# LSH attention and an MLP on one core: transfers and weight loads as one server in the planner, and a new table of priorities

## The chip, the cores and the metric

One core of a Trainium2 chip runs the whole program in one launch. The metric is the device time of an execution in microseconds. TensorE is written PE, VectorE DVE, ScalarE ACT, GpSimd POOL; SyncE (SP) issues most transfers.

## The reference

q, k and v have the shape (4, 8, 768, 64): 4 batches, 8 heads. Each row of q and k gets a bucket from the signs of 6 projections; a query sees only the keys of its own bucket. The heads' outputs stand side by side as 3072 tokens of 512 numbers, which go through a two-layer MLP.

```python
q_bucket = sum((q @ proj > 0) * 2**arange(6));  k_bucket likewise
mask   = q_bucket[:, None] == k_bucket[None, :]
scores = where(mask, (q @ k.T) / 8, -1e9)
attn   = softmax(scores) @ v                  # by batch and head
x      = attn as (3072, 512)
r      = maximum(x @ w_in, 0)                 # w_in 512 x 2048
out    = (s * r*r + b) @ w_out                # w_out 2048 x 512
```

## The kernel before

Attention goes by visits, one for each batch and head (32), and each visit by three chunks of 256 queries: 96 slots. For each slot PE makes scores of all 768 keys (L657 or L659, the "lead"), DVE takes the maxima (L665), PE transposes them (L676, first 24 slots only), DVE reduces them (L678), PE transposes once more (L680), DVE writes the row of maxima (L687), and PE adds mask and maxima to the scores (L697 or L699, the "rest"). ACT takes the exponentials (L704), PE multiplies them with v (L727, or L729 and L730), ACT brings the result out of PSUM (L767, L769). Bank 4 of PSUM serves the transposes L676 and L680 and also the preparation of later visits: transposes of q and k (L477, L491), hashes (L515, L528 to L533), sums of v (L579, L615). None of these may write it until DVE has read what stands there.

Visits 0, 1, 4 and 7 (heads of mode "a" and "b") need no transfers between preparation and scores. The others do: after the hash (L533 or L529) DVE makes the bits (L545) and SP issues four transfers inside SBUF (`aq<-bq`, `bq<-aq`, `ks<-nat`, `aq<-nat`), and the lead L659 waits for the last. Two heads done, a quarter of a token's features goes to DRAM (`xd<-xsb`) and comes back laid out for the MLP (`xc<-xd`, L802).

The MLP (L815 and L832) of a chunk can start when all 8 heads of the chunk are there, from slot 23 on. From then on PE has matmuls that wait for nothing in attention. The weights come in as 32 loads of 512 KB on ACT's queue (`raw<-in_moe_w...`, L392), and in the first 28 slots ACT, DVE and POOL split each into two parts (L393 to L405).

No engine chooses at run time: each runs its instructions in a written order. That order comes from a planner in the file, `Plan.order`. Every step is added with an engine, a cost, what it reads and writes, a priority `pr`, and a `lag` after which its result can be used. The planner plays the engines forward by these costs and at each point takes the ready step of lowest priority number. `NUDGE` adds a number to the priority of each source site (91 of them) in each of up to five stretches of the program (`CUTS`). In the model before, SP's transfers follow each other on one server (`moved`), and ACT's weight loads are outside it: they take 0.1 us of ACT and land 5.0 us later, whatever else is under way.

Of the kernel before, what the change touches and what calls it, by code (L numbers as in the profile page):

```python
# [31 lines left out]
class Plan:  # L32
# [41 lines left out]
    def order(self):  # L74
        n = len(self.steps)
        sites = sorted({s[2].__code__.co_firstlineno for s in self.steps})
        pr = []
# [32 lines left out]
        while len(out) < n:  # L110
# [33 lines left out]
            if e == SP:  # L144
                moved = max(moved, start + cost) + lag
                end += moved - start - cost
            else:
                end += lag
# [28 lines left out]
HOP = {None: 0.0, PE: 0.2, DVE: 0.06, ACT: 0.06, POOL: 0.06, SP: 1.8}  # L177
SAME = {None: 0.0, PE: 0.2, DVE: 0.06, ACT: 0.06, POOL: 0.06, SP: 0.0}
# [10 lines left out]
def lsh_attention_moe(ctx: ExitStack, tc, q, k, v, proj, w_in, w_out, s, b, out):  # L189
# [34 lines left out]
    def dma(dst, src, r, w, pr, size=0):  # L224

        plan.add(SP, 0.7, lambda: nc.sync.dma_start(f32(dst()), f32(src())), r, w, pr, size / 2.6e5)
# [144 lines left out]
    def decode(u, pr):  # L371
# [20 lines left out]
        plan.add(ACT, 0.1, lambda: nc.scalar.dma_start(raw(), src.rearrange("p (n t) -> p n t", t=2)), KK("a") if u < PACE else [], rk + [("pace", u % PACE)], pr - 5, 5.0)  # L392
# [41 lines left out]
    def load(w, pr):  # L434
# [3 lines left out]
        if w >= BT:  # L438
            flat = NAT[x].rearrange("p t j d -> p (t j d)")
            for j in range(4):  # L440
                to = flat[j * SQ:(j + 1) * SQ].rearrange("r (t m e) -> r t m e", t=NT, e=SQ)
                z = (q, k)[j // 2][bb, h].rearrange("(m r t) (j e) -> j r t m e", r=SQ, t=NT, e=SQ)[j % 2]
                plan.add(SP, 0.7, lambda to=to, z=z: nc.sync.dma_start(to, z), [], [("nat", x, j)], pr, 0.9)
            return
        for j, z in enumerate((q, k)):
            to = NAT[x][:, :, j]
            plan.add(SP, 0.7, lambda to=to, z=z: nc.sync.dma_start(to, z[bb, h].rearrange("(p t) d -> p t d", t=NT)), [], [("nat", x, j)], pr, 0.9)
# [112 lines left out]
    def prep_values(w, pr):  # L560
# [4 lines left out]
        if w < NPL:  # L565
# [5 lines left out]
            plan.add(SP, 0.7, lambda: nc.sync.dma_start(EV[x][:, :, 0], vd), [], vk[0:1], pr, 0.9)  # L571
# [26 lines left out]
        def fetch(to, tk, vd):  # L598
            plan.add(SP, 0.7, lambda: nc.sync.dma_start(to, vd), [], [tk], pr, 0.9)
# [190 lines left out]
    def moe(bb, c):  # L790
        boxes = []
        pr = 1e5 + 100.0 * nu[0]
        for cc in range(NC_):
# [8 lines left out]
            plan.add(SP, 0.7, lambda box=box, src=src: nc.sync.dma_start(f32(box["t"]), f32(src)), [("xd", (bb, cc, c))], [("xc", r)], pr, 262144 / 2.6e5)  # L802
# [103 lines left out]
PACE = 2  # L906
# [130 lines left out]
```

## Time and profile before

| | us |
|---|---|
| median of 3 runs | 987.71 |
| lowest, highest | 985.8, 988.32 |
| the profiled execution's own time | 984.95 |
| its span, first to last instruction | 983.2 |

The busy shares are PE 98%, PEld (loading of PE's weights, beside PE) 88%, DVE 71%, ACT 72%, POOL 69%. The profile's rows give busy time by engine, windows of it, waits with what ended them, and the chain of work that ended last. A matmul of the exact heads (L657, and L727 of the first 27 slots) shows as two records in the trace for one instruction in the order.

### The profile page before, as it was taken

The numbers are of one execution on the slowest core, as the hardware profiler recorded it, in microseconds if no ns is written. First come the engines' busy times: TensorE is split into PE (matmuls) and PEld (weight loads), VectorE is DVE, ScalarE is ACT, GpSimd is POOL, SyncE is SP. The second block draws the span as 40 slices with busy tenths as digits, with TensorE's granted clock in tenths as the row PEclk, the third lists the DMA queues.
The fourth block names the chain that finished last, engine by engine and source line by source line (L and its number), as shares of the span: only waits on it lengthen the run. The fifth ranks groups of instructions, "written<-read, shape, count | busy, mean of one in ns | idle before, by whom it ended". The sixth has DMA issues, their size and how long they took to land.

```text
span 983.2 us, 17823 instructions
## 1 busy us (share of the span) xinstructions
PE 958.6 (98%) x6322; PEld 863.4 (88%) x6322; DVE 699.3 (71%) x1081; ACT 703.8 (72%) x1365; POOL 680.2 (69%) x641
## 2 busy tenths in 40 slices
PE   8999878999999999999999999999999999999998
PEld 7877667789999999999999999999999999989997
DVE  6678678878888898888898888888888876100000
ACT  4777667768888787878788788878887877433332
POOL 3677766588878786978788787869788788422222
PEclk9999999999999999999999999999999999999999
DMA  7574765642433442533433433533523310201100
GB/s 189 140 208 136 187 148 160 173 89 57 122 93 75 103 116 60 135 83 73 122 85 82 102 100 70 138 80 83 136 64 73 116 36 11 87 23 43 33 22 22
DMA packets 133680, 95.21 MB, mean 97 GB/s; under 512 B 101464, under 2 KB 106328, under 8 KB 133592
## 3 DMA queue, kind: packets, MB, share of 16 engines
q1 hardware_dynamic: 128248, 77.03, 31.2%
q10 hardware_dynamic: 5344, 17.05, 5.5%
q8 instruction: 50, 0.82, 0.3%
q14 instruction: 38, 0.31, 0.1%
HBM read 50.40 MB, written 18.87 MB: 70 GB/s over the span
## 4 chain that ended last, share of the span: by engine, by line
PE 94%; ACT 2%; DVE 2%; DMA 1%; issue 1%; POOL 0%; DVEq 0%; ACTq 0%; SPq 0%; POOLq 0%
PE bank L815 28%; PE bank L832 27%; PE bank L659 7%; PE bank L727 6%; PE bank L699 6%; PE bank L729 5%; PE bank L730 5%; PE bank L657 3%; PE bank L680 1%; PE bank L762 1%; PE bank L528 1%; PE bank L529 1%; PE bank L697 1%; ACT ex L704 1%; PE bank L515 1%
## 5 line engine op out<-in xcount | busy, mean ns | idle before, releaser
L815 PE MATMUL bank<-xc,w 128*128 128x256 f32 x2304 | 341.7, 283 | 0.0
L723 POOL TENSOR_TENSOR hl<-et,hl 128x512 fp32r<-128x512 f32 x207 | 267.5, 1320 | 82.3 <-ACT hl L722 73.3
L815 PEld LDWEIGHTS bank<-xc,w 128*128 128x128 f32 x2304 | 309.4, 190 | 8.2
L832 PE MATMUL bank<-w,ghb 128*128 128x512 f32 x768 | 251.8, 397 | 0.0
L823 POOL TENSOR_TENSOR glb<-rb,ghb 128x512 fp32r<-128x512 f32 x96 | 124.7, 1299 | 106.6 <-ACT ghb L822 97.5
L665 DVE TENSOR_REDUCE mx<-bank 128x256 f32<-128x1536 f32 x96 | 167.9, 1749 | 8.2 <-PE bank L659 4.8
L704 ACT ACTIVATE et<-bank 128x512 f32<-128x512 f32 x234 | 129.2, 626 | 49.8 <-PE bank L699 31.1
L749 DVE TENSOR_REDUCE zb<-et 128x256 f32<-128x1536 f32 x69 | 120.7, 1750 | 48.0 <-ACT et L704 43.9
L832 PE MATMUL bank<-w,glb 128*128 128x512 f32 x384 | 152.5, 398 | 0.0
L832 PEld LDWEIGHTS bank<-w,ghb 128*128 128x128 f32 x768 | 134.3, 189 | 17.8
L722 ACT CAST hl<-et 128x512 fp32r<-128x512 f32 x207 | 125.4, 668 | 0.3
L820 ACT ACTIVATE rb<-bank 128x512 f32<-128x512 f32 x96 | 56.9, 593 | 89.6 <-PE bank L815 88.8
L659 PE MATMUL bank<-aq,ks 84*128 84x256 f32 x504 | 110.1, 304 | 4.4 <-DMA aq<-nat 3.3
L729 PE MATMUL bank<-hl,vs 128*128 128x256 f32 x414 | 109.0, 286 | 0.0
L730 PE MATMUL bank<-hl,vs 128*128 128x256 f32 x414 | 107.4, 282 | 0.0
L659 PEld LDWEIGHTS bank<-aq,ks 84*128 84x128 f32 x504 | 80.1, 191 | 12.0 <-ACT w L399 3.0
L729 PEld LDWEIGHTS bank<-hl,vs 128*128 128x128 f32 x414 | 78.0, 188 | 7.9
L832 PEld LDWEIGHTS bank<-w,glb 128*128 128x128 f32 x384 | 72.3, 188 | 13.8 <-POOL glb L823 0.2
L730 PEld LDWEIGHTS bank<-hl,vs 128*128 128x128 f32 x414 | 78.4, 189 | 6.6
L769 ACT ACTIVATE xpb<-bank,vmn 64x256 f32<-64x256 f32 x96 | 44.9, 468 | 49.5 <-PE bank L730 29.8
L840 DVE SCALAR_TENSOR_TENSOR osb<-bank,misc,bcs 128x512 f32<-128x512 f32 x22 | 16.2, 743 | 89.4 <-PE bank L832 89.1
L699 PE MATMUL bank<-bq,ks 128*128 128x256 f32 x504 | 76.7, 287 | 0.0
(144 smaller groups left out, 1571.1 us busy)
## 6 DMA issues: line engine op xcount, KB each, us to landing
xd<-xsb SPq DMA_DIRECT2D x48, 256.0 KB
xc<-xd SPq DMA_DIRECT2D x48, 256.0 KB
raw<-in_moe_w_in_dram ACTq DMA_DIRECT2D x16, 512.0 KB
raw<-in_moe_w_out_dram ACTq DMA_DIRECT2D x16, 512.0 KB
vn<-in_v_dram SPq DMA_DIRECT2D x34, 192.0 KB
out_dram<-osb SPq DMA_DIRECT2D x22, 256.0 KB
ks<-aq SPq DMA_DIRECT2D x28, 192.0 KB
ks<-bq SPq DMA_DIRECT2D x28, 192.0 KB
```

The source lines that it names most:

```text
L659: nc.tensor.matmul(o, ks[0:HR + NR, 0, kt], aq[0:HR + NR, cs], start=m == 0, stop=m == 1, skip_group_check=True)
L665: dve(S * TPC, lambda: nc.vector.tensor_reduce(t, sc, AX.XY, ALU.max), [("b", b) for b in pb], [tk], pr, 1.75)
L699: nc.tensor.matmul(o, ks[:, 1, kt], bq[:, cs], start=False, stop=m == 1, skip_group_check=True)
L704: act(512, lambda p=p, z=z: nc.scalar.activation(et(z) if plain(i) else pairs(z), bank[:, pb[p]] if plain(i) else bank[:, pb[p]].rearrange ...
L722: act(512, lambda z=z, y=y: nc.scalar.copy(HL[2 * y].rearrange("p (m n) -> p m n", n=CH), pairs(z)), [("e", z)], [("hl", 2 * y)], pr, 0.05)
L723: pool(512, lambda z=z, y=y: nc.gpsimd.tensor_tensor(HL[2 * y + 1].rearrange("p (m n) -> p m n", n=CH), pairs(z), f32(HL[2 * y]).rearrange ...
L729: nc.tensor.matmul(av, VS[x][:, kt], HL[2 * y][:, ms], start=(kt == 0), stop=False)
L730: nc.tensor.matmul(av, VS[x][:, kt], HL[2 * y + 1][:, ms], start=False, stop=(kt == NT - 1))
L749: dve(S * TPC, lambda: nc.vector.tensor_reduce(ZB, es, AX.XY, ALU.add), [("e", z) for z in range(NE)], ["zb"], pr, 1.75)
L815: nc.tensor.matmul(hp, wt[("wi", n, cc)][:, m % 2, fs], xc[:, m // 2, :], start=(cc == 0 and m == 0), stop=(cc == NC_ - 1 and m == 2))
L823: pool(2 * CH, lambda r=r, gh=gh, gl=gl: nc.gpsimd.tensor_tensor(gl, r, f32(gh), ALU.subtract), [rk, hk], [lk], MP)
L832: nc.tensor.matmul(bank[:, 6 + t, :], (gh, gh, gl)[n][:, ts], wt[("wo", f)][:, n % 2], start=(f == 0 and n == 0), stop=(f == NF - 1 and n ...
```

## The change

In the planner, a step with a lag, on whatever queue, now passes one server: `moved` runs on by the step's lag, and the result is there 1.3 us (`LAND`) after. Costs and lags of all transfers are new numbers: of a weight load 0.33 us to issue and 2.2 us of service, of a 256 KB transfer 0.45 us and about 0.78 us, of the small ones 0.36 to 0.7 us and 0.7 to 1.1 us. The table `NUDGE` has other values at nearly every place. Nothing else differs: the same instructions with the same operands, in another order. The line numbers of the changed file are smaller by one.

```diff
             free[e] = start + cost
             end = start + cost + HOP[e]
-            if e == SP:
+            if lag:
                 moved = max(moved, start + cost) + lag
-                end += moved - start - cost
-            else:
-                end += lag
+                end = moved + LAND
...
+LAND = 1.3
...
     def dma(dst, src, r, w, pr, size=0):
-        plan.add(SP, 0.7, lambda: nc.sync.dma_start(f32(dst()), f32(src())), r, w, pr, size / 2.6e5)
+        plan.add(SP, 0.45 if size > 2e5 else 0.68, lambda: nc.sync.dma_start(f32(dst()), f32(src())), r, w, pr, size / (3.4e5 if size > 2e5 else 2.5e5) + 0.01)
...
-        plan.add(ACT, 0.1, lambda: nc.scalar.dma_start(raw(), src.rearrange("p (n t) -> p n t", t=2)), KK("a") if u < PACE else [], rk + [("pace", u % PACE)], pr - 5, 5.0)
+        plan.add(ACT, 0.33, lambda: nc.scalar.dma_start(raw(), src.rearrange("p (n t) -> p n t", t=2)), KK("a") if u < PACE else [], rk + [("pace", u % PACE)], pr - 5, 2.2)
...
 NUDGE = {
-    0: {0: -3.8, 1: -12.8, 2: 5.9, 3: 23, 4: -30},
+    0: {0: 30, 1: -20.8, 2: 7.3, 3: -18.6, 4: -8.3},
...
```

Three places show what moves. The first is PE, from the second hash of visit 6 (batch 0, head 6; its tiles are `aq1`, `bq1`, `ks1`) to its first lead. `eva`, `vs5` are values of visits 4 and 5, `ks0` the keys of visit 5, `nat1` holds q and k of visit 7. Before:

```order
L533 MATMUL bank_64<-bq1_71,pjs_134 24x384
L727 MATMUL bank_64<-et_81,vs5_793 128x256 x3
L676 MATMUL bank_64<-ident_117,mx_88 128x128 x2
L727 MATMUL bank_64<-et_81,vs5_793 128x256
L680 MATMUL bank_64<-ident_117,nmt_93 8x128
L477 MATMUL bank_64<-ident_117,nat1_67 128x128 x3
L699 MATMUL bank_64<-bq0_70,ks0_72 128x256 x6
L659 MATMUL bank_64<-aq1_69,ks1_73 128x256 x2
```

In the changed kernel (L532 is before's L533, and so on):

```order
L532 MATMUL bank_64<-bq1_71,pjs_134 24x384
L658 MATMUL bank_64<-aq0_68,ks0_72 128x256 x6
L726 MATMUL bank_64<-ex5_87,eva_75 128x256
L675 MATMUL bank_64<-ident_117,mx_88 128x128 x2
L679 MATMUL bank_64<-ident_117,nmt_93 8x128
L726 MATMUL bank_64<-et_81,vs5_804 128x256 x2
L698 MATMUL bank_64<-bq0_70,ks0_72 128x256 x2
L578 MATMUL bank_64<-misc_102,vn_74 64x1
L698 MATMUL bank_64<-bq0_70,ks0_72 128x256 x4
L726 MATMUL bank_64<-et_81,vs5_804 128x256 x4
L675 MATMUL bank_64<-ident_117,mx_88 128x128 x2
L658 MATMUL bank_64<-aq1_69,ks1_73 128x256 x6
```

Between hash and lead there are now seven value matmuls where there were four, and six leads of visit 5 that stood earlier. The transposes of `nat1` (L477), which stood directly behind L680, are gone from here; two value matmuls stand behind L679.

The second is ACT in the same stretch: the weight loads 21 and 22 (`raw21`, `raw22`) and the exponentials (`ex0` to `ex2`) of slot 16. Before:

```order
L392 DMA raw21_235<-in_moe_w_out_dram 128x1024
L393 ACTIVATE osb_101<-raw20_234 128x512
L769 ACTIVATE xpb_96<-bank_64,vmn_92 64x256
L394 ACTIVATE raw20_234<-raw20_234 128x512
L767 ACTIVATE zpb_91<-bank_64 64x256
L392 DMA raw22_236<-in_moe_w_out_dram 128x1024
L480 ACTIVATE eqb_78<-bank_64,misc_102 128x384
L704 ACTIVATE ex0_82<-bank_64 128x512
L704 ACTIVATE ex1_83<-bank_64 128x512
L704 ACTIVATE ex2_84<-bank_64 128x512
L399 CAST w19_1197<-osb_101 128x512
L480 ACTIVATE eqb_78<-bank_64,misc_102 128x384
```

In the changed kernel:

```order
L391 DMA raw21_235<-in_moe_w_out_dram 128x1024
L398 CAST w18_1172<-osb_101 128x512
L703 ACTIVATE ex0_82<-bank_64 128x512
L557 ACTIVATE vmn_92<-bank_64 64x1
L703 ACTIVATE ex1_83<-bank_64 128x512
L703 ACTIVATE ex2_84<-bank_64 128x512
L392 ACTIVATE osb_101<-raw20_234 128x512
L768 ACTIVATE xpb_96<-bank_64,vmn_92 64x256
L398 CAST w19_1198<-osb_101 128x512
L766 ACTIVATE zpb_91<-bank_64 64x256
L393 ACTIVATE raw20_234<-raw20_234 128x512
L391 DMA raw22_236<-in_moe_w_out_dram 128x1024
```

Load 22 stood ahead of the three exponentials, with four instructions between it and load 21; now it stands behind them, with ten between. A copy of a weight (L398) now stands ahead of the exponentials and a mean (L557) among them.

The third is PE where the MLP starts, in slots 23 and 24 (`xc0_0_0` to `xc0_0_3` are the four parts of the first chunk). Before:

```order
L815 MATMUL bank_64<-xc0_0_0_240,w0_364 128x256 x3
L815 MATMUL bank_64<-xc0_0_1_241,w1_398 128x256 x3
L815 MATMUL bank_64<-xc0_0_2_242,w2_432 128x256
L727 MATMUL bank_64<-ex4_86,evb_76 128x256 x2
L680 MATMUL bank_64<-ident_117,nmt_93 8x128
L727 MATMUL bank_64<-ex5_87,evb_76 128x256 x2
L815 MATMUL bank_64<-xc0_0_2_242,w2_432 128x256 x2
L699 MATMUL bank_64<-bq0_70,ks0_72 128x256 x6
L528 MATMUL bank_64<-aq1_69,pjs_134 56x384
L529 MATMUL bank_64<-bq1_71,pjs_134 24x384
L815 MATMUL bank_64<-xc0_0_3_243,w3_461 128x256 x2
L659 MATMUL bank_64<-aq0_68,ks0_72 128x256 x2
```

In the changed kernel:

```order
L814 MATMUL bank_64<-xc0_0_0_240,w0_356 128x256 x3
L814 MATMUL bank_64<-xc0_0_1_241,w1_397 128x256 x3
L814 MATMUL bank_64<-xc0_0_2_242,w2_447 128x256 x3
L726 MATMUL bank_64<-ex3_85,evb_76 128x256 x2
L726 MATMUL bank_64<-ex4_86,evb_76 128x256 x2
L726 MATMUL bank_64<-ex5_87,evb_76 128x256
L679 MATMUL bank_64<-ident_117,nmt_93 8x128
L726 MATMUL bank_64<-ex5_87,evb_76 128x256
L698 MATMUL bank_64<-bq0_70,ks0_72 128x256 x6
L527 MATMUL bank_64<-aq1_69,pjs_134 56x384
L528 MATMUL bank_64<-bq1_71,pjs_134 24x384
L658 MATMUL bank_64<-aq0_68,ks0_72 128x256 x2
```

Before, the first MLP matmuls stood in four places among attention's; now nine stand together, and the next, which read `xc0_0_3`, come after 14 rows of attention.

## Rows read from the trace of the kernel before

**Rows 1.** The page, busy time by engine: us (share of the span), instructions.

```profile
...
PE 958.6 (98%) x6322; PEld 863.4 (88%) x6322; DVE 699.3 (71%) x1081; ACT 703.8 (72%) x1365; POOL 680.2 (69%) x641
```

**Rows 2.** Windows: length, busy us (instructions) by engine, PEclk, DMA share, GB/s.

```profile
...
8.00:185.00 177.00, 157.49 (x839) 126.14 (x837) 135.84 (x209) 126.61 (x252) 117.13 (x114) 0.99 0.62 169
185.00:979.00 794.00, 793.96 (x5444) 730.62 (x5442) 557.88 (x842) 575.68 (x1112) 560.12 (x518) 1.00 0.31 80
979.00:984.00 5.00, 0.38 (x2) 0.00 (x0) 1.23 (x3) 0.00 (x0) 0.00 (x0) 0.82 0.30 105
```

**Rows 3.** Waits of TensorE, 8 to 185 us: total us, times, longest.

```profile
...
PE bank L659 <- DMA aq<-nat: 3.3, 2, 2.8
PE bank L697 <- DVE zhl L687: 2.5, 4, 1.1
PE bank L727 <- ACT ex L704: 2.4, 4, 1.4
PE bank L579 <- DVE bq L687: 1.4, 3, 0.6
PE bank L680 <- DVE nmt L678: 1.2, 3, 0.5
...
PE bank L477 <- DVE bq L687: 1.2, 2, 0.6
...
PE bank L515 <- DVE bq L687: 0.7, 2, 0.5
...
PE bank L657 <- ACT ex L704: 0.6, 2, 0.3
...
PE bank L491 <- DVE bq L687: 0.5, 1, 0.5
```

**Rows 4.** Chain that ended last, 110 to 117 us: start, us, what.

```profile
...
113.50 2.43 DMA aq<-nat
...
116.06 0.95 PE bank L659 x6
```

**Rows 5.** The same chain, 124 to 136 us.

```profile
...
125.22 0.18 PE bank L533
...
126.69 0.23 PE bank L676 x2
...
128.10 4.03 DMA aq<-nat
...
132.37 0.77 PE bank L659 x2
```

**Rows 6.** Timeline of ScalarE, 124 to 133 us: start, us, instruction.

```profile
...
127.39 0.33 ACTq L392 DMA_DIRECT2D raw<-in_moe_w_out_dram  x1
...
129.46 1.56 ACT L704 ACTIVATE ex<-bank 128x512 f32<-128x512 f32 x3
```

**Rows 7.** Windows around the wait in rows 5 (columns as in rows 2).

```profile
...
123.00:127.30 4.30, 4.30 (x25) 3.47 (x23) 3.60 (x6) 3.21 (x6) 2.14 (x3) 1.00 0.71 198
127.30:132.40 5.10, 1.59 (x12) 1.19 (x11) 2.48 (x6) 4.08 (x8) 3.21 (x3) 0.99 0.58 158
132.40:135.80 3.40, 3.40 (x12) 3.04 (x13) 1.95 (x2) 1.39 (x3) 1.21 (x2) 0.51 0.55 87
```

**Rows 8.** Lines of ScalarE, 8 to 185 us: count | busy us, mean ns | idle before.

```profile
...
L399 ACT CAST w<-osb 128x512 fp32r<-128x512 f32 x28 | 17.3, 618 | 3.1 <-POOL osb L397 3.1
...
L769 ACT ACTIVATE xpb<-bank,vmn 64x256 f32<-64x256 f32 x23 | 10.8, 468 | 15.7 <-PE bank L727 15.5
...
L521 ACT COPY eka<-eqa 12x768 f32<-12x768 f32 x2 | 1.7, 828 | 0.4 <-DVE eqa L517 0.3
```

**Rows 9.** Lines of VectorE, 8 to 185 us.

```profile
...
L517 DVE TENSOR_SCALAR eqb<-bank,misc 44x384 f32<-44x384 f32 x4 | 2.7, 670 | 2.4 <-PE bank L515 2.3
```

**Rows 10.** The same chain, 190 to 195 us, back-to-back matmuls.

```profile
...
190.37 1.08 PE bank L815 x9
...
191.90 2.76 PE bank L727 x12
```

More of the change, by code (lines that the diff above doesn't have):

```diff
@@ L442, in load @@
                 z = (q, k)[j // 2][bb, h].rearrange("(m r t) (j e) -> j r t m e", r=SQ, t=NT, e=SQ)[j % 2]
-                plan.add(SP, 0.7, lambda to=to, z=z: nc.sync.dma_start(to, z), [], [("nat", x, j)], pr, 0.9)
+                plan.add(SP, 0.68, lambda to=to, z=z: nc.sync.dma_start(to, z), [], [("nat", x, j)], pr, 0.7)
             return
@@ L446, in load @@
             to = NAT[x][:, :, j]
-            plan.add(SP, 0.7, lambda to=to, z=z: nc.sync.dma_start(to, z[bb, h].rearrange("(p t) d -> p t d", t=NT)), [], [("nat", x, j)], pr, 0.9)
+            plan.add(SP, 0.7, lambda to=to, z=z: nc.sync.dma_start(to, z[bb, h].rearrange("(p t) d -> p t d", t=NT)), [], [("nat", x, j)], pr, 1.0)
     nfill = [0]
@@ L570, in prep_values @@
                 pool(1, lambda: nc.gpsimd.memset(EV[x][:, :, 1], 1.0), [], vk[1:2], pr, 0.5)
-            plan.add(SP, 0.7, lambda: nc.sync.dma_start(EV[x][:, :, 0], vd), [], vk[0:1], pr, 0.9)
+            plan.add(SP, 0.6, lambda: nc.sync.dma_start(EV[x][:, :, 0], vd), [], vk[0:1], pr, 1.1)
             if w > 1:
@@ L598, in fetch @@
         def fetch(to, tk, vd):
-            plan.add(SP, 0.7, lambda: nc.sync.dma_start(to, vd), [], [tk], pr, 0.9)
+            plan.add(SP, 0.36, lambda: nc.sync.dma_start(to, vd), [], [tk], pr, 0.8)
         def sums(j, to, tk):
@@ L801, in moe @@
             src = xd[(bb, cc, c)]
-            plan.add(SP, 0.7, lambda box=box, src=src: nc.sync.dma_start(f32(box["t"]), f32(src)), [("xd", (bb, cc, c))], [("xc", r)], pr, 262144 / 2.6e5)
+            plan.add(SP, 0.36, lambda box=box, src=src: nc.sync.dma_start(f32(box["t"]), f32(src)), [("xd", (bb, cc, c))], [("xc", r)], pr, 1.0)
             boxes.append((box, ("xc", r)))
```

180 rows, old and new, of the table NUDGE are left out of this document.

## Prediction

> **What bounds the kernel now.** I read the page first: PE is busy for 98% of the span, the other engines for about 70% [rows 1], so PE is the bound on average. The windows say where it isn't. From 185 us, when the MLP has started, to 979 us PE is idle for 794.00 - 793.96 = 0.04 us [rows 2]; no order of the same matmuls gains there, and one only loses if it opens a gap. From 8 to 185 us, batch 0 of attention, PE is idle for 177.00 - 157.49 = 19.5 us [rows 2], while no other engine is busy for more than 136 of the 177 us: no engine is full, each waits for another in turn. So the change is worth what it does to these 19.5 us, and to one stretch after a wait in which PE ran at the lower of its two clock levels. The view of the waits splits the 19.5: 3.3 us for a transfer, 7.5 us for DVE's steps behind the transposes of bank 4 (2.5 + 1.4 + 1.2 + 1.2 + 0.7 + 0.5), 3.0 us for exponentials (2.4 + 0.6) [rows 3], the rest in small pieces. The chain shows where the transfer is late, the windows around it what the clock then did.
>
> **The change part by part.** The instructions are the same, so nothing is saved or added in work; only waits change. The planner's costs act through the order alone, and I judge them by what the order now puts between a producer and its user, in PE time by the durations of records: 0.12 us for a score or MLP matmul, 0.23 us a record and two records, so 0.46 us, for a value matmul of an exact head [rows 10].
>
> *The transfer behind the hash.* Visit 6's second hash ends at 125.22 + 0.18 = 125.40 us, its first lead starts at 132.37 [rows 5]: 6.97 us, filled with 3.2 us of PE work in the order (four value matmuls 1.84, two transposes 0.23 [rows 5], the rest of visit 5 0.72, four short transposes about 0.4). The last transfer took 4.03 us [rows 5], the same transfer of visit 5 took 2.43 us [rows 4]. What differs is weight load 22, issued at 127.39 us [rows 6], 0.71 us ahead of it. In the new order that load stands behind the exponentials of slot 16, which began at 129.46 us [rows 6] in the old run, so the small transfer should be nearer to 2.43: the way takes 6.97 - 1.60 = 5.4 us. PE's filling becomes 5.3 us (seven value matmuls 3.2, twelve score matmuls 1.4, transposes and a sum 0.7). Left: 0.1 of 2.8 us. Visit 5's wait was the other 0.5 us of the 3.3 [rows 3]; its filling goes from about 4.0 to 6.2 us in the order, so it goes. Gain 3.2 us; at best 3.3, at worst 0, if the next late thing (below) ends in the same place.
>
> A rule of the Trainium skill speaks against the planner's picture here. In "DMA: Bandwidth & Descriptors", section "Queues, rings and completion order", each DMA engine takes turns between the queues it has work for, packet by packet; SP's transfers then share with a load of ACT's queue, and don't stand behind the whole of it as the one server has them. The trace can't settle it: sharing would be the 1.6 us between 2.43 and 4.03; a server would make the small transfer wait for 512 KB at 198 GB/s [rows 7], 2.6 us, less the 0.71 already gone, 1.9 us. By the one the term is as above, by the other 0.3 us larger, which is not there to be gained. So the rule changes no sum at this place.
>
> *The clock.* After that wait PE's granted clock is 0.51 for 3.4 us [rows 7], the 1.2 GHz level; before it PE had been idle for 5.10 - 1.59 = 3.5 us of 5.1. PE is busy all through it, so half of it is lost: 1.7 us. With no long wait ahead of it I take the whole 1.7; at worst 0, or another such stretch elsewhere (+1.7).
>
> *Bank 4.* Behind L680 the row of maxima must be written before a bank-4 step or the rest may run. In the order of the first 24 slots, such a step stands directly behind L680 in 9 slots before (0, 8, 11, 15 to 18, 21, 22) and in 4 now (0, 6, 7, 10); L680 directly behind L676 in 2 before (0, 18), in 3 now (0, 16, 20). The waits for L687 are 2.5 + 1.4 + 1.2 + 0.7 + 0.5 = 6.3 us [rows 3], those of L680 for L678 1.2 [rows 3]. Scaled by the places they become 6.3 x 4/9 = 2.8 and 1.2 x 3/2 = 1.8: gain 3.5 - 0.6 = 2.9 us. Best 3.5, worst 0, when another input of the same step ends as late.
>
> *Exponentials.* Two counts oppose each other. Value matmuls with under 1 us of PE work since the rest they depend on: 9 slots before, 3 now, which scales the 3.0 us to 1.0, a gain of 2.0. But ACT has 20 other instructions between the three exponentials of a slot where it had 8, over 24 slots; scaled by those the 3.0 us become 7.5, a loss of 4.5. PE's own waits are nearest to the first count, ACT's queue to the second: I take 0 and keep both ends.
>
> *The start of the MLP.* Nine of its matmuls run, then 14 rows of attention stand alone, some 7.5 us by the durations above. PE is idle 11% of batch 0 (19.5 of 177), so 0.8 us is lost there; 0 to 1.5.
>
> *Visit 7.* Between its second hash and its first lead PE has 2.3 us of work, where it had 10.3. The way is 0.67 on DVE [rows 9] and 0.83 on ACT [rows 8] behind an exponential that itself takes some 0.6 (1.56 for three [rows 6] at closer spacing): 2.1 us and the hops. I take 0.3 lost; up to 1.8 when a queued step on DVE and on ACT come first (0.6 each [rows 8]).
>
> All other edits are priced at nothing: from visit 9 on every hash has over 13 us of PE work ahead of its lead in both orders (25 us from visit 12 on), so a later landing is hidden by the MLP. Were that cover gone, each visit would pay what visit 6 paid, 2.8 us.
>
> **The sum.** -3.2 - 1.7 - 2.9 + 0 + 0.8 + 0.3 = -6.7 us. Against the profiled execution, 984.95 us (a span of 983.2 and 1.75 around it), that is 978.3. That execution is 2.76 us below the median of the runs, 987.71, and below all three; runs of the changed kernel will be compared by medians, so the forecast is 987.71 - 6.7 = 981.0.
>
> **Rivals.** *The gain is given back at the next wait.* In the stretch of the long wait ACT is busy for 4.08 of 5.10 us [rows 7]: it is what comes late next, and PE's value matmuls wait for its exponentials instead of the transfer. Likewise behind L680. Then the clock's 1.7 and, as I choose, a fourth of the 3.2 are left: -2.5, 985.2. For it: all engines but PE are at 70% or more in batch 0, each PE wait there is short, and 19.5 us are spread over many places. Against: the order adds filling at nearly every place named.
>
> *ACT's queue turns it round.* The 12 further instructions ahead of exponentials cost PE what they last: six are L769 at 0.47 us [rows 8], and at that mean 12 make 5.6 us. And an L769 waits for PE's values: 15.7 us of idle time for 23 of them [rows 8], 0.68 each, 4.1 for six, during which the exponentials behind it stand. 9.7 us, all on PE's path if the filling doesn't cover it: 987.71 - 6.7 + 9.7 = 990.7. It decides from 6.7 us on, two thirds of it. Against: rest to value matmul has more PE work between than before in most slots, which is just what would cover a later exponential.
>
> *More than I count.* The shorter waits of batch 0 that I priced at nothing (19.5 - 3.3 - 7.5 - 3.0 = 5.7 us) shrink as the bare places of bank 4 do (11 in all become 7), by 4/11, 2.1 us, and the exponentials by their 2.0: -10.8, 976.9.
>
> *The planner's server is the wrong picture.* If queues share the engines, the order guards against delays that aren't there, and the costs are as good or bad as the old ones: 987.7, no change; it adds to the first rival's chance.
>
> **How the numbers follow.** Forecast (978 to 984.5) 0.50; more 0.12; given back, or the planner's picture worthless, 0.23; turned round 0.15. A measurement of this kernel can tell 0.3%, 3 us, from no change. The forecast and the larger gain are over that, save a little at the upper end: faster 0.63. Of the third case most lies within: same 0.22. Slower 0.15. The range leaves out the upper part of the turned case and the far end of the large gain: 975.5 to 989.
>
> **What would show it.** In the profile of the changed kernel: windows from 8 us to the start of the MLP with about 14 us of PE idle instead of 19.5; no wait of L658 for `aq<-nat` above 0.5 us; the granted clock at 1.00 throughout batch 0; the waits for DVE's L686 and L677 about 5 us. The forecast is wrong if waits of PE for L703 grow past 6 us, if the wait at visit 6 is there again under another name, or if a gap opens behind the start of the MLP.

## The result and the profile after

The changed kernel takes 999.85 us (median of 4 runs, 999.45 to 1001.34), the kernel before 988.02 (median of 4, 985.8 to 989.03): ratio 1.0114, 95% interval 1.010 to 1.0128. It is slower by 1.1%; 981.0 was forecast. Its profiled execution took 999.85 us with a span of 998.1; that of before was a low one (984.95), so the profiles differ by 14.9 us where the medians differ by 11.8.

Busy time by engine from the page after, beside [rows 1]:

```profile
PE 967.3 (97%) x6322; PEld 869.4 (87%) x6322; DVE 700.6 (70%) x1081; ACT 708.8 (71%) x1365; POOL 678.8 (68%) x641
```

PE's idle time is 998.1 - 967.3 = 30.8 us, 983.2 - 958.6 = 24.6 before: +6.2. PE is busy 8.7 us longer over the same matmuls. Windows of the changed kernel, first those of [rows 2], then four stretches at the lower clock:

```profile
8.00:185.00 177.00, 156.12 (x820) 125.34 (x820) 128.12 (x199) 122.80 (x241) 111.09 (x108) 0.97 0.62 164
185.00:979.00 794.00, 789.11 (x5378) 724.51 (x5377) 566.35 (x849) 580.60 (x1118) 560.83 (x521) 1.00 0.32 81
...
119.70:123.10 3.40, 3.40 (x14) 2.75 (x12) 1.43 (x4) 1.91 (x4) 2.59 (x4) 0.50 0.96 260
153.70:157.10 3.40, 3.40 (x9) 2.56 (x9) 0.00 (x0) 2.94 (x6) 3.32 (x3) 0.52 0.21 58
181.20:188.00 6.80, 6.39 (x22) 5.06 (x21) 4.17 (x8) 3.38 (x7) 4.04 (x4) 0.50 0.38 60
205.00:208.40 3.40, 3.40 (x12) 2.90 (x11) 1.41 (x2) 2.68 (x5) 2.56 (x2) 0.50 1.10 235
```

In these four stretches, 17.0 us in all, PE ran at the 1.2 GHz level; before had one of 3.4 [rows 7]. PE was busy for 16.6 of the 17.0 us, and half of that is lost: 8.3 against 1.7, +6.6 us of the 8.7. The last 2.1 us I can't place.

Waits of TensorE from 8 to 185 us, beside [rows 3]:

```profile
PE bank L658 <- DMA vn<-in_v_dram: 3.8, 1, 3.8
PE bank L658 <- ACT ex L703: 3.4, 5, 1.3
PE bank L578 <- POOL vn L576: 3.2, 1, 3.2
PE bank L679 <- DVE nmt L677: 1.6, 3, 0.6
...
PE bank L658 <- DMA aq<-nat: 0.8, 1, 0.8
PE bank L578 <- DVE bq L686: 0.7, 1, 0.7
PE bank L490 <- DVE zhl L686: 0.6, 1, 0.6
PE bank L698 <- DVE bq L686: 0.5, 1, 0.5
PE bank L530 <- DVE bq L686: 0.5, 1, 0.5
...
PE bank L656 <- ACT et L703: 0.3, 1, 0.3
```

The wait at visit 6 (L658 for `aq<-nat`) is down to 0.8 us. The waits of 3.8 and 3.2 us are new, and neither is at a place that the prediction priced. The first is at 150 us: L578 sums the values of visit 8 (`vs8`), which landed late. The chain there, and what SP's and ACT's queues issued around it:

```profile
144.79 7.16 DMA vs<-in_v_dram
```

```profile
144.12 0.58 SPq L442 DMA_DIRECT2D nat<-in_k_dram  x1
144.79 0.65 SPq L570 DMA_DIRECT2D vs<-in_v_dram  x1
```

```profile
144.59 0.33 ACTq L391 DMA_DIRECT2D raw<-in_moe_w_out_dram  x1
144.96 0.53 ACTq L391 DMA_DIRECT2D raw<-in_moe_w_in_dram  x1
```

Weight loads 23 and 24 went out 0.2 us before and 0.2 us after the values, which took 7.16 us. The second is at 176 us, at visit 8's first lead. The profile names `vn`, the latest transfer; the lead reads `aq0`. SP itself waits for that transfer before it may load `nat` anew, so its queue shows the landing:

```profile
173.58 0.72 SPq L225 DMA_DIRECT2D aq<-nat  x1
...
180.24 0.69 SPq L442 DMA_DIRECT2D nat<-in_q_dram  x1
```

From 173.58 to 180.24: 6.66 us, with loads 27 and 28 issued at 170.56 and 170.92. In both places two loads stand directly behind one another in ACT's order. The changed kernel has six such pairs (1, 7, 18, 20, 24 and 28 follow directly on another), before had two (1 and 3). Behind each wait PE's clock is low, for 3.4 and 6.8 us.

The same place in the kernel before shows that the pair alone doesn't make the difference. There loads 27 and 28 went out only 0.46 us apart, with steps of ACT between them in the order, and the hash transfer followed 3.7 and 3.2 us behind them:

```profile
169.33 0.33 ACTq L392 DMA_DIRECT2D raw<-in_moe_w_in_dram  x1
...
169.79 0.36 ACTq L392 DMA_DIRECT2D raw<-in_moe_w_out_dram  x1
```

```profile
172.99 0.78 SPq L226 DMA_DIRECT2D aq<-nat  x1
177.73 1.43 SPq L443 DMA_DIRECT2D nat<-in_q_dram  x2
```

It landed within 4.7 us, and PE had work meanwhile. From the end of visit 8's second hash to its first lead, before and in the changed kernel (columns as in [rows 2]):

```profile
169.13:177.82 8.69, 8.11 (x41) 6.41 (x40) 8.36 (x14) 5.96 (x12) 4.21 (x4) 1.00 0.67 179
```

```profile
169.68:180.39 10.71, 6.73 (x34) 5.18 (x34) 7.35 (x11) 5.97 (x12) 2.96 (x3) 1.00 0.89 223
```

So two things changed at visit 8's hash: the landing takes 1.9 us longer or more, and PE has 1.4 us less work to hide it.

### The profile page after: what moved, and what is told of

It reads as the page before. It is cut to its first block, busy times and chain, and to the rows that moved or that the text cites. A ratio compares the mean times of both kernels' runs of the same rounds, so it can differ in the third digit from the quotient of the medians.

```text
span 998.1 us, 17862 instructions
## 1 busy us (share of the span) xinstructions
PE 967.3 (97%) x6322; PEld 869.4 (87%) x6322; DVE 700.6 (70%) x1081; ACT 708.8 (71%) x1365; POOL 678.8 (68%) x641
## 4 chain that ended last, share of the span: by engine, by line
PE 83%; DMA 6%; DVE 3%; POOL 3%; ACT 3%; issue 1%; SPq 1%; ACTq 0%; DVEq 0%; POOLq 0%
PE bank L814 25%; PE bank L831 25%; PE bank L658 6%; PE bank L698 5%; PE bank L728 5%; PE bank L729 5%; PE bank L726 4%; PE bank L656 2%; DMA vs<-in_v_dram 1%; DMA vn<-in_v_dram 1%; DMA xd<-xsb 1%; PE bank L679 1%; PE bank L761 1%; POOL osb L396 1%; PE bank L528 1%
## 5 line engine op out<-in xcount | busy, mean ns | idle before, releaser
L814 PE MATMUL bank<-xc,w 128*128 128x256 f32 x2304 | 335.0, 283 | 0.6 <-DMA xc<-xd 0.6
L814 PEld LDWEIGHTS bank<-xc,w 128*128 128x128 f32 x2304 | 305.9, 190 | 8.1 <-DMA xc<-xd 0.8
L703 ACT ACTIVATE et<-bank 128x512 f32<-128x512 f32 x234 | 129.8, 626 | 42.5 <-PE bank L698 29.9
L721 ACT CAST hl<-et 128x512 fp32r<-128x512 f32 x207 | 127.9, 665 | 0.5
L658 PE MATMUL bank<-aq,ks 84*128 84x256 f32 x504 | 110.1, 305 | 9.8 <-ACT ex L703 4.6
L728 PE MATMUL bank<-hl,vs 128*128 128x256 f32 x414 | 107.0, 284 | 0.0
L729 PE MATMUL bank<-hl,vs 128*128 128x256 f32 x414 | 106.2, 281 | 0.0
L658 PEld LDWEIGHTS bank<-aq,ks 84*128 84x128 f32 x504 | 80.7, 192 | 19.3 <-ACT ex L703 6.8
L698 PE MATMUL bank<-bq,ks 128*128 128x256 f32 x504 | 79.7, 290 | 2.4 <-DVE bq L686 2.3
```

The lines of the kernel that those rows point to most:

```text
L658: nc.tensor.matmul(o, ks[0:HR + NR, 0, kt], aq[0:HR + NR, cs], start=m == 0, stop=m == 1, skip_group_check=True)
L698: nc.tensor.matmul(o, ks[:, 1, kt], bq[:, cs], start=False, stop=m == 1, skip_group_check=True)
L703: act(512, lambda p=p, z=z: nc.scalar.activation(et(z) if plain(i) else pairs(z), bank[:, pb[p]] if plain(i) else bank[:, pb[p]].rearrange ...
L721: act(512, lambda z=z, y=y: nc.scalar.copy(HL[2 * y].rearrange("p (m n) -> p m n", n=CH), pairs(z)), [("e", z)], [("hl", 2 * y)], pr, 0.05)
L728: nc.tensor.matmul(av, VS[x][:, kt], HL[2 * y][:, ms], start=(kt == 0), stop=False)
L729: nc.tensor.matmul(av, VS[x][:, kt], HL[2 * y + 1][:, ms], start=False, stop=(kt == NT - 1))
```

## The experiments

Theory A: the loss is these two landings and the clock behind them, and they are late because of the paired loads. Rivals: it is lost wherever the model sets landings too early; or what is saved at one wait is lost at the next. The experiments on the changed kernel move single steps in the order that the planner returns, by a few lines behind `queue = plan.order()`: `at(line, n)` is step n, counted from 0, of those written at that line, and `move(a, b)` puts a directly behind b, which is on the same engine. Their definitions are left out of the code shown, and so is a sorting step that some runs have behind the moves and that leaves each engine's order as it is.

**One load away from visit 8's values.**

```diff
     queue = plan.order()
+    move(at(391, 24), at(703, 57))
```

> The changed kernel, with weight load 24 alone issued later, behind the first exponential of its slot. In the changed kernel load 23 was issued 0.20 us before the values of visit 8 (144.59 and 144.79 us), load 24 0.17 us after them (144.96), and the values took 7.16 us to land; PE then waited 3.2 us for their sum, and its clock fell for 3.4 us. Theory (queues share the engines): a load issued after the values slows them too, so the values land in 4.5 to 5.5 us, PE's wait shrinks by 1.5 to 2.5 us or goes with the dip behind it: 1.5 to 4 us faster than the changed kernel's 999.85, about 996 to 998.5. Rival (one server, first come first served, as the plan has it): a load issued after the values cannot delay them; 7.2 us again, the wait again 3 us, 999 to 1001. Rival (the loss is ACT's queue of exponentials, not transfers): no change in time either, but the landing may shorten.

Measured: 996.63 us, ratio 1.0075 (1.0059 to 1.0092). The profiled execution is the slowest of the four (999.2 us; behind the later wait at visit 8's hash its clock is low for 10.2 us), so the time is read from the median, and only the landing and the wait from the trace. Chain and wait of PE:

```profile
144.75 5.67 DMA vs<-in_v_dram
```

```profile
PE bank L578 <- POOL vn L576: 1.7, 1, 1.7
```

One load less, and the landing falls from 7.16 to 5.67 us, though that load had been issued behind the values. So it isn't a server that takes transfers in the order of issue.

**Both loads away.**

```diff
+    move(at(391, 24), at(703, 57))
+    move(at(391, 23), at(392, 22))
```

> The changed kernel with load 24 later as before and load 23 earlier, behind the first decode step of load 22, so that no weight load is issued beside the values of visit 8. Theory (transfers piled on each other make the loss): the values land in 2.5 to 4 us, PE's 3.2 us wait and the clock's half of 3.4 us go: 4 to 5 us faster than the changed kernel, 995 to 996. Rival (one server): the same here, since load 23 was ahead of the values. Rival (ACT's queue of exponentials): no change, 999 to 1001.

Measured: 995.75 us, ratio 1.0069 (1.0054 to 1.0084), -4.1 us. Beside no load the values, issued at 144.79 us, were there after 3.9 us, and PE's wait is all but gone:

```profile
148.72 0.64 POOL L574 TENSOR_TENSOR vn<-vs 128x192 f32<-128x192 f32 x1 [2.36 <-DMA vs<-in_v_dram]
```

```profile
PE bank L578 <- POOL vn L576: 0.2, 1, 0.2
```

**Both loads away from visit 8's hash transfers.**

```diff
+    move(at(391, 28), at(398, 26))
+    move(at(391, 27), at(703, 68))
```

> The changed kernel with weight loads 27 and 28 later: 27 behind the exponentials of the slot, 28 behind the next weight copy. They were issued at 170.56 and 170.92 us, 3.0 and 2.7 us ahead of the transfer aq<-nat of visit 8, for which PE waited 3.8 us, with the clock low for 6.8 us after. Theory: the transfer lands in 2.5 to 4 us, the wait and at least half of the low clock go: 5.5 to 7 us faster than the changed kernel's 999.85, 993 to 994.5. Rival (the pile is SP's own: eight transfers issued from 168.6 to 175.9 us): the wait shrinks by less than 1.5 us, 997 to 999. Rival (ACT's queue): no change.

Measured: 991.77 us, ratio 1.0028 (1.0013 to 1.0043), -8.1 us, more than expected: the whole low stretch of 6.8 us went with the wait. SP could load `nat` 2.3 us after the last hash transfer's issue:

```profile
173.19 0.72 SPq L225 DMA_DIRECT2D aq<-nat  x1
...
175.48 0.68 SPq L442 DMA_DIRECT2D nat<-in_q_dram  x1
```

**The prediction's own reason, on the kernel before:** load 22 behind the exponentials of slot 16, where the change put it.

```diff
     queue = plan.order()
+    move(at(392, 22), at(704, 50))
```

> The kernel before with weight load 22 alone moved behind the three exponentials of slot 16, as in the changed kernel. The prediction priced this transfer's wait at visit 6 at 2.8 us and the low clock after it at 1.7: if that is right, 3.5 to 4.5 us faster than before, 983.5 to 984.5 against 988, with aq<-nat landing in about 2.4 us. Rival (the time is given back at the next wait, for ACT): 1 to 2.5 us faster, 985.5 to 987. Rival (the transfer is slow for another reason): no change, landing 4.0 us again.

Measured: 987.88 us, ratio 0.9991 (0.9977 to 1.0006): no gain. The transfer of [rows 5] took as long as before, and PE's wait was longer:

```profile
131.01 4.01 DMA aq<-nat
```

```profile
PE bank L659 <- DMA aq<-nat: 6.1, 3, 5.0
```

By the profile SP first waits for three transfers `ks<-aq` to land, 5.5 us here and 3.4 in before, so the hash transfers went out later. The moved load went out at 130.34 us, 0.67 us ahead of the last of them, as near as before (0.71). So the run shows that moving load 22 alone gains nothing. It doesn't show whether a load beside it made that transfer slow, since the load stayed beside it. (The traced execution, 991.01 us, is the slowest of its ten.)

**Both corrections at once.**

```diff
+    move(at(391, 24), at(703, 57))
+    move(at(391, 23), at(392, 22))
+    move(at(391, 28), at(398, 26))
+    move(at(391, 27), at(703, 68))
```

> The changed kernel with both corrections at once: weight loads 23 and 24 apart (load 23 behind the decoding of raw22, load 24 behind the first exponential of slot 19) and loads 27 and 28 apart (behind the third exponential of slot 22, and behind the copy of w26). Alone they gave -4.1 and -8.1 us. Theory A (two separate late landings, each from two weight loads beside a small transfer): the two add up, 999.85 - 12.2 = 987.7 us, ratio to before 0.9995; the 3.2 us wait of L578 for vn and the 3.8 us wait of L658 for aq<-nat are both gone, and the granted clock stays at full level from 150 to 190 us. Rival (one loss passed on: what is saved at one place is lost at the next wait): under -9 us, 991 or more.

Measured: 989.2 us, ratio 1.0008 (0.9989 to 1.0026). Both at once gain 10.7 us, against 12.2 one by one. The ten runs spread from 985.94 to 995.4, so the 1.5 between them can't be told from noise. The loss is gone, both waits are (0.2 us is left for L578), and the clock is at its full level from 150 to 190 us. Four of the six pairs of loads still stand, so a pair by itself costs nothing. But nothing is won either. Its windows:

```profile
8.00:185.00 177.00, 161.41 (x867) 129.96 (x866) 136.65 (x217) 130.51 (x257) 118.01 (x114) 0.99 0.63 169
185.00:979.00 794.00, 789.65 (x5407) 726.36 (x5407) 557.21 (x832) 576.56 (x1107) 558.27 (x518) 1.00 0.31 80
```

PE is idle for 15.6 us of batch 0 where it was 19.5 [rows 2], so 3.9 of the forecast's gain is there; behind 185 us it is idle for 4.35 us where it was 0.04. So the gain was given back, 3.3 of the 4.35 us in the first 20 us of the MLP. The longest piece is at 200 us, seen on PE, ACT and SP:

```profile
202.20 0.50 PE L658 MATMUL bank<-aq,ks 84*128 84x256 f32 x2 [2.19 <-ACT ex L703]
```

```profile
199.33 0.41 ACT L779 CAST xsb<-xpb 128x256 fp32r<-128x256 f32 x1 [3.34 <-DMA xd<-xsb]
```

```profile
191.43 1.40 SPq L442 DMA_DIRECT2D nat<-in_q_dram  x2
192.88 1.35 SPq L442 DMA_DIRECT2D nat<-in_k_dram  x2
194.32 6.57 SPq L225 DMA_DIRECT2D xd<-xsb  x2
```

Exponentials stand behind L779, L779 waits for `xd<-xsb`, and that stands behind four loads of `nat` on SP, though `xsb` was written at 191.5 us. Two ways to mend it were run.

**Exponentials ahead of L779** (the four moves, and):

```diff
+    move(at(703, 80), at(821, 0))
+    move(at(703, 80), at(821, 0))
+    move(at(703, 80), at(821, 0))
```

> As the run with both corrections, and on ACT the exponentials ex3 to ex5 of slot 26 stand ahead of L779, which waits 3.5 us at 200 us for xsb to be read by xd<-xsb (SP issues that transfer behind four loads of nat). Theory A: the 2.4 us wait of L658 for the exponentials at 204 us goes too, 987.7 - 2.4 = 985.3 us, ratio to before 0.997. Rival (the feature transfer xd is itself on the path, so that PE waits for the MLP's input or for the values behind L768 instead): 987 to 989 us, no change from the run without it.

Measured: 990.04 us, ratio 1.0011 (0.9998 to 1.0025): no change, as the rival had it, if a little above its range. PE's wait for exponentials went, and PE waited 1.4 us for L766, which now stood behind them.

**The transfer ahead of the four loads** (the four moves, and):

```diff
+    move(at(225, 60), at(225, 59))
```

> The changed kernel with both corrections, and on SP the transfer xd<-xsb of slot 25 stands ahead of the four loads of nat (q and k of visit 10) that it stood behind. In the run with both corrections xsb is written at 191.5 us, the transfer is issued at 194.3 and L779 on ACT waits 3.3 us for it until 199.3, with the exponentials of slot 26 behind it, for which PE waits 2.2 us at 200 us. Theory A (that wait is the same kind of late landing: a short transfer behind other transfers): the wait of L779 goes, the wait of L658 at 200 us falls under 0.5 us, -2 us against the run with both corrections, so 987.2 us by the last median, ratio to before 0.998. Rival (the four loads, now later, make DVE's transposes of nat late, or ACT is simply full there): no change, ratio 1.0005 to 1.002.

Measured: 986.27 us, ratio 0.9975 (0.9965 to 0.9985): 0.25% faster than the kernel before, with 1 outside the interval. L779 no longer waits, and PE's idle time behind 185 us is 2.8 us (in the fastest of the twelve runs, which is the profiled one):

```profile
194.53 0.40 ACT L779 CAST xsb<-xpb 128x256 fp32r<-128x256 f32 x1
```

```profile
185.00:979.00 794.00, 791.21 (x5411) 727.02 (x5409) 557.93 (x833) 576.12 (x1104) 558.43 (x517) 1.00 0.31 80
```

**Model and table apart.** The new model with the old table, and the old model with the new table (the two hunks of the diff exchanged).

> One part alone: the planner's new model (one server for all transfers, new issue and service times) with the old table of priorities. In this order only loads 0 and 1 stand directly behind one another on ACT; in the order before there are two such pairs, in the changed kernel six. Theory A (the loss of the changed kernel lies in the pairs beside small transfers, not in the model as such): no wait of over 3 us for a transfer between 140 and 185 us, 986 to 993 us. Rival B (the new model's landings, 1.3 us behind the service, are too early everywhere, so any order by it loses): 996 us or more. Rival C (the model is better and only the table's search went wrong): below 985 us.

> The other part alone: the old model with the new table of priorities. Three pairs of loads stand directly behind one another (1, 3, 28). Theory A: the table was made for another model, so steps stand in places that neither search chose; no forecast of its own beyond: a wait of 3 to 4 us for a transfer where loads 27 and 28 are paired, and with that and no other 990 to 996 us. Rival B (the table alone carries the loss of the changed kernel): 998 us or more. Rival C (the table is as good as the old one): 986 to 989 us.

Measured: 1014.92 (ratio 1.0263, 1.024 to 1.0287) and 1014.9 us (1.0262, 1.0244 to 1.028). The numbers of both rivals B came true, but not as an account of the changed kernel's loss: each part alone loses 2.6%, more than the two together with 1.1%, so the loss can't be laid on one of them. That a table serves only the model it was made for would explain it and was not tested. In neither run is there a wait of 3 us for a transfer between 140 and 185 us, though loads 27 and 28 are paired in the second. PE is idle 1012.7 - 973.0 = 39.7 us in the first, in many pieces, and busy 14.4 us longer than before:

```profile
PE 973.0 (96%) x6322; PEld 866.0 (86%) x6322; DVE 706.9 (70%) x1081; ACT 703.8 (70%) x1365; POOL 680.5 (67%) x641
```

**Is it the number of loads?** The kernel before with 512 KB more on ACT's queue, behind load 24 and, as a control, behind load 25.

```diff
+        def load():
+            nc.scalar.dma_start(raw(), src.rearrange("p (n t) -> p n t", t=2))
+            if u == 24:
+                nc.scalar.dma_start(tc.dram_tile([P, 1024], I32, name="again"), src)
...
```

> The kernel before, with one extra 512 KB transfer (the same weights, from DRAM to a piece of DRAM that nothing reads) on ACT's queue directly behind weight load 24, which is issued with the values of visit 8 at 144.9 us. Order and work are else those of before. In before the values landed 4.9 us after their issue (POOL L575 at 149.84), beside one load; PE waited 0.5 us for L577. Theory A (each weight load beside a small transfer makes it later by about 1.6 us): the values land 6.5 to 7.2 us after issue, PE's wait for L577 grows to 2.1 to 2.8 us, with a dip of the clock behind it (1.7 us) in all +2 to +4.5 us, ratio 1.002 to 1.0045. Rival (in the changed kernel it was the order around that place, not the second load): landing under 5.3 us, ratio 0.999 to 1.001.

> Control: the same extra transfer in the kernel before, but behind weight load 25, issued at 149.1 us when the values of visit 8 have nearly landed. Theory A: landing of the values and PE's wait for L577 as in before (4.9 and 0.5 us), 0 to +1 us in all, ratio 0.999 to 1.001. Rival (any further 512 KB of traffic in batch 0 costs the same, wherever it stands): as the run with the extra transfer behind load 24, +2 us or more.

Measured: 987.98 (ratio 0.9994, 0.9983 to 1.0005) and 989.61 us (1.0006, 0.9995 to 1.0017). Theory A missed: with the extra transfer, out 0.4 us behind them, the values were issued at 145.54 us and landed at 150.35, 4.8 us, as before:

```profile
145.93 0.60 ACTq L395 DMA_DIRECT2D again<-in_moe_w_in_dram  x1
```

```profile
150.35 0.59 POOL L579 TENSOR_TENSOR vn<-vs 128x192 f32<-128x192 f32 x1 [2.65 <-DMA vs<-in_v_dram]
```

So 512 KB more beside a transfer don't make it late in every case. (They went to DRAM, a weight load goes to SBUF; whether that matters was not tried.) Before has nothing of `nat` shortly ahead of the values in SP's queue: the last went out by 137.8 us. Two runs left the pairs and changed only what stands ahead on SP.

**The values of visit 8 ahead of the fourth load of `nat`.**

```diff
     queue = plan.order()
+    move(at(570, 8), at(225, 40))
```

> The changed kernel, both pairs of loads where they are (23 and 24, 27 and 28), but on SP the values of visit 8 stand one place earlier, ahead of the fourth load of nat (128-byte rows). In the changed kernel they landed 7.16 us after issue; with one weight load less 5.67, with none 3.9; but in the kernel before an extra 512 KB behind the load left the landing at 4.8 us. Theory B (what a weight load costs a short transfer is set by what stands ahead of it in SP's own queue, above all the 128-byte rows, which crawl beside a load): issue 0.67 us earlier, landing 4.2 to 5.2 us after issue, PE's wait of 3.2 us at 150 us gone or under 0.5 us, the dip of the clock behind it gone; -3 to -4.5 us, 995.5 to 997 us, ratio to before 1.007 to 1.0085. Theory A (each load beside costs about 1.6 us, whatever is ahead): landing about 7 us, PE waits 2.5 us, under -1 us.

Measured: 995.89 us, ratio 1.0078 (1.0062 to 1.0094), -4 us. Issued at 144.04, there at 149.37 (5.3 us, a little over what was expected), both loads beside it. PE's wait at 150 us is down from 3.2 to 0.7 us, also a little over, and the low clock behind it is gone:

```profile
149.00:153.00 4.00, 3.34 (x20) 2.71 (x18) 2.99 (x4) 3.62 (x8) 3.40 (x5) 1.00 0.66 202
```

The move did two things: it took one load of `nat` from ahead of the values, and it brought the values 0.4 and 0.8 us ahead of both weight loads, where they had gone out between them. The run doesn't tell the two apart. That 128-byte rows crawl beside a load is part of theory B; no run shows it by itself.

**`xd<-xsb` behind visit 8's hash transfers.**

```diff
     queue = plan.order()
+    move(at(225, 49), at(225, 53))
```

> The changed kernel, both pairs of loads where they are, but on SP the 256 KB transfer xd<-xsb of visit 7 stands behind the four transfers of visit 8's hash, of which the last (aq<-nat) PE waits 3.8 us for at 176 us. Theory B (what stands ahead in SP's own queue sets the price): 256 KB less ahead, the last transfer is issued 0.4 us earlier and lands 5 to 5.8 us after issue instead of 6.6, PE's wait falls to 1.5 to 2.5 us; -1.5 to -4 us with the dip behind it, if that goes. Theory A: landing 6.3 us or more, the wait stays over 3.2 us, within -0.8 us.

Measured: 1000.67 us, ratio 1.0115 (1.0098 to 1.0132): nothing. The last hash transfer took from 172.85 to 180.29 us, 7.4 us, and PE waited 4.1:

```profile
172.85 0.73 SPq L225 DMA_DIRECT2D aq<-nat  x1
...
180.29 0.68 SPq L442 DMA_DIRECT2D nat<-in_q_dram  x1
```

Theory B, that what stands ahead in SP's queue sets the price, fits the values and misses at the hash, as far as this one transfer of 256 KB goes. Here too the move brought the transfer nearer to the two loads: 2.5 and 2.2 us behind them instead of 3.0 and 2.7.

**One load beside the hash instead of two.**

```diff
     queue = plan.order()
+    move(at(391, 28), at(398, 26))
```

> The changed kernel with load 28 alone moved away (behind the copy of w26); load 27 stays where it is, 3 us ahead of the last hash transfer of visit 8 (aq<-nat), which landed 6.6 us after issue beside both loads and made PE wait 3.8 us. Theory A (the two loads' traffic sets it, each with its own part): landing 4.3 to 5.5 us, PE's wait 1.5 to 2.8 us, -1 to -5 us (with the dip of the clock of 6.8 us behind the wait shortened by half), 995 to 998.9 us, ratio to before 1.007 to 1.0105. Theory C (only the pair does it, by the second load that follows directly on the first; one load beside is free, as in the kernel before with its values): wait under 0.7 us and no dip, -7 to -8.5 us as with both loads moved, 991.5 to 993 us, ratio 1.003 to 1.0045. Theory D (one load is enough): within 1 us of the changed kernel.

Measured: 997.38 us, ratio 1.0089 (1.0054 to 1.0123). The four runs go from 995.07 to 1001.23 us, so by time alone this can't be told from the changed kernel. The landing, the wait and the low clock behind it (3.4 us instead of 6.8) are as theory A had them. The profile names `ks<-nat`, another of the hash transfers, for the wait:

```profile
174.69 0.72 SPq L225 DMA_DIRECT2D aq<-nat  x1
...
179.56 0.69 SPq L442 DMA_DIRECT2D nat<-in_q_dram  x1
```

```profile
PE bank L658 <- DMA ks<-nat: 2.1, 1, 2.1
```

In the changed kernel with no, one and two loads the last hash transfer lands after at most 2.3, after 4.9 and 6.7 us, and PE waits 0, 2.1 and 3.8 us. At the values it was 3.9, 5.7 and 7.2 us. Shown is that at both places the transfer is on time when the loads are taken away, and late by a part with one of them. The number of loads isn't the whole price: with the same two, the hash transfer of the kernel before landed within 4.7 us, and with two the values landed in 5.3 us when they went out ahead of them. A rival that no run separates from what stands ahead in SP's queue is how far apart in time the loads and the transfer go out. What exactly sets the price stays open.

## Why the prediction was wrong

*"All other edits are priced at nothing ... from visit 9 on every hash has over 13 us of PE work ahead."* This step failed. It looked at hashes from visit 9 on and left out visit 8, where the order has less PE work between the hash and its lead than before: 6.1 us against 7.4 by the planner's costs, 6.7 against 8.1 in the traces. And it asked only for PE work between a hash and its lead, not for what now goes out beside a transfer. Taken away, the two late landings at visit 8 gave 4.1 and 8.1 us one by one and 10.7 both at once, of a loss of 11.8. The order had the six pairs in view; I read ACT's order at one place only.

Visit 8 is 10.7 of the 18.9 us between the forecast of 981.0 and the result. With both landings mended 989.2 is still 8.2 over the forecast. The largest parts of that are the start of the MLP and the clock, below.

*The transfer behind the hash, -3.2.* The waits shrank nearly as said, from 2.8 and 0.5 us to 0.8, but not by a shorter way:

```profile
129.92 2.97 DMA aq<-nat
...
133.14 0.94 PE bank L658 x6
```

The hash ended at 125.80 us and the lead started at 133.14, so the way was 7.3 us where it had been 7.0 and 5.4 was forecast. PE's longer filling hid it. The last transfer by itself did get shorter, 2.97 us against 4.03, with no load issued in the 2.7 us ahead of it. That agrees with the reason that I gave, but the run that should have tested it, on the kernel before, left the load as near to the transfer as it was. So the reason stays open.

By the Trainium skill ("DMA: Bandwidth & Descriptors", section "Queues, rings and completion order") each DMA engine takes turns between the queues. The runs at visit 8 agree: a load issued 0.17 us after the values still delayed them (7.16 us with it, 5.67 without). I weighed that rule at visit 6 only, where it changes no sum, and didn't ask what it means at the other places.

*The clock, -1.7.* It had the wrong sign: +6.6. Each of the two new waits was followed by a low stretch, the second by one of 6.8 us. With the landings mended the mean granted clock of the profiled run is back at 0.998. But the 1.7 us was not gained then either. One low stretch of 3.4 us is left, now at 119.7 us (119.5 in that run), behind two waits for ACT (L490 1.0 and L658 1.2 us in the changed kernel) where before had none of over 0.2: the "another such stretch elsewhere" of the prediction.

*Bank 4, -2.9.* Right: the waits for L686 and L677 are 1.6 + 0.7 + 0.6 + 0.5 + 0.5 = 3.9 us where they were 7.5, -3.6.

*Exponentials, 0.* PE's waits for L703 grew by about 0.9 us, well within the ends: 3.4 + 0.4 + 0.3 + 0.2 = 4.3 against 3.4, which is the 3.0 of [rows 3] and two waits of 0.2 that it leaves out.

*Visit 7, +0.3.* No wait of PE shows between its second hash (148.66 us) and its first lead (155.40) that visit 7 itself makes; the 3.2 us for visit 8's values fall there. The wait of 0.3 us of L656 for ACT is at another place, before 140 us.

*The start of the MLP, +0.8, at most 1.5.* Mis-sized: 4.3 us with the two landings mended. I scaled with batch 0's idle share; the longest piece, 2.2 us, was one transfer behind four others on SP. This gave back what bank 4 and visit 6 had gained, so that without the loss at visit 8 the change would have been worth nothing: the rival "given back at the next wait", at another place than I put it.

*Server the wrong picture.* That rival had no change, and was too mild. The changed file's planner doesn't take a pair of loads for free: it gives each 2.2 us of the server. But in its own times (`plan.start`) neither late transfer has one of the paired loads ahead of it. The values of visit 8 go out 2.1 us before load 23, and the last hash transfer 1.5 us before load 27. (It plans 0.16 us of service for that transfer, less than the 0.7 to 1.1 given above for small ones.) In the run load 23 went out 0.2 us before the values and load 27 3.0 us before the hash transfer. The landings that it plans for them, 3.5 and 2.1 us, are near those measured with none beside (3.9, at most 2.3). So what failed there is less the landing than the order in time between two queues, which the written order doesn't fix. Why the run's times drifted so far from the plan's was not looked into.

## What to carry to other kernels

Read a new order by the queues too: for every transfer that an engine soon waits for, see what now stands beside it in other queues and ahead of it in its own. A written order fixes what each engine issues after what, but not when two queues issue beside each other: check in a trace where the plan's distances hold, and keep work between a transfer and its user for the case that a large load comes beside it. What is lost by one late landing is the wait and, behind it, the clock.

## What was not expected of the hardware

A 512 KB load issued 0.2 us behind a transfer of the other queue made it land 1.5 us later (7.16 against 5.67 us), while 512 KB more, 0.4 us behind the same transfer in the kernel before, moved its landing not at all (4.8 against 4.9).

Nor does the time at the lower clock follow the length of the wait ahead of it. Behind the wait at visit 8's hash PE's clock was low for 6.8 us in the changed kernel (wait 3.8), for 3.4 with one load (2.1), and for 10.2 with the values moved ahead (4.0) and with load 24 alone moved (3.5), the first 1.4 and 1.6 us of these still within the wait. With the values moved ahead:

```profile
174.50:185.00 10.50, 8.35 (x27) 6.67 (x28) 4.67 (x9) 3.55 (x8) 4.51 (x4) 0.52 0.36 58
```
